# Down and output projections as seven products with tokens as the weights of TensorE

## The chip, the cores and the metric

The kernel runs on one core of one Trainium2 chip. The metric is device time in microseconds (us) of one execution. Engines are named as in the profile: PE is TensorE (PEld its weight loads), DVE is VectorE, ACT is ScalarE, POOL is GpSimd, SP the engine that issues the DMAs. A "product" below is one matmul instruction of PE: it multiplies a *stationary* block (128x128, loaded as weights) by a *moving* block of 128 rows and up to 512 columns and adds the result to a bank of PSUM.

## The reference

One transformer block on 2048 tokens of width 640, attention and a gated MLP side by side on the same normalised input:

```python
xn = layernorm(x)
q, k, v = split(xn @ wqkv)                 # 32 heads of 20
p = softmax(mask(q k^T / sqrt(20)))        # causal, window of 256 keys
o = p v                                    # heads joined: 640 columns
h = gelu(xn @ w_gate) * (xn @ w_up)        # 1728 columns
out = x + o @ wo + h @ w_down
```

All is float32. The kernel keeps float32 accuracy on PE by splitting each operand into a high part (rounded to the type fp32r) and a low part (the rest), and adding three products: high by high, high by low, low by high. One "term" below is such a set of three.

## The kernel before, in words

The work has three stages, one after the other in time, with PE busy through all of them.

- **Stage 1 (to about 658 us)**: layer norm, q, k and v, attention, and the first gate and up tiles as filler. Each unit of attention leaves its unnormalised output in DRAM (`od[c]`, 640 rows by 512 tokens, `av_unit`, L492) and the softmax sums in `sd[c]` (32 heads by 512 tokens). There are four chunks `c` of 512 tokens.
- **Stage 2 (658 to 843 us)**: the other gate and up tiles, `gate_up_pair` (L846), which already forms its products from sums of blocks (seven products in place of eight). Its list `extra` takes small jobs that are hung in between its product groups (`more(i)`, L852). Results go to DRAM as `hd[f]`: tile f (128 hidden features) by 512 tokens. During this stage the softmax sums are inverted and split into three bfloat16 parts (`norm_items`, L997), which are kept in SBUF as `rp`.
- **Stage 3 (843 us to the end)**: down and output projection. The loop of L1092 goes over 4 chunks of 512 tokens and, within a chunk, over 14 tiles of `hd` and 5 tiles of `od`, 19 steps in all. The *weights are stationary*: for each of the five blocks of 128 output columns, `terms` (L940) multiplies 128x128 blocks of `wd` or `wo` (high and low) by 512 moving token columns and adds into one of five PSUM banks (`ps_w`). The output is thus transposed (columns by tokens), and the host turns it back.

What sets the order in stage 3: SP issues the DMAs in the program's order (`MANUAL_OUT`, L41); the other engines are scheduled. A step n is loaded three steps ahead (`load_step`, L906, tile `hr`) and split two steps ahead (`split_step`, L920): ACT makes the high part of 128x512 (L932), POOL the low part (L934). For an attention step PE first spreads the inverted sums over the rows by a product with 0/1 weights `sel` (L925, `ps_b`), DVE multiplies (L927), ACT takes the high part (L928), DVE the low part (L929). The weights of the 19 tiles are loaded one a step during the first chunk and split once, ACT high (L76) and DVE low (L77); they then stay in SBUF. At the end of a chunk DVE adds the input `xt` and SP stores (L961, L962).

The last two weight tiles' preparation in stage 2 (`down`, L1018) and the splits of steps 0 and 1 are hung into the last gate and up tile (f = 12) by `second` (L1072 to L1074).

Of the kernel before, what the change touches and what calls it, by code (L numbers as in the profile page):

```python
# [9 lines left out]
F32 = mybir.dt.float32  # L10
# [9 lines left out]
C = 512  # L20
# [4 lines left out]
NF = 14  # L25
# [9 lines left out]
NDA = 2  # L35
# [8 lines left out]

@with_exitstack
def block_kernel(ctx, tc, x, xt, wqk, wv, wo, wgu, wd, wdl, out):
# [16 lines left out]
    xh = xp.tile([128, KT, S], F32R, name="xh")  # L63
    xl = xp.tile([128, KT, S], F32R, name="xl")
# [5 lines left out]
    td = [{i: dram.tile([128, 2, C], F32, name=f"td{p}{i}") for i in (1, 2, 3, 4)} for p in range(NC // 2)]  # L70
    hd = [dram.tile([NC, 128 if f < NF - 1 else 64, C], F32, name=f"hd{f}") for f in range(NF)]
# [21 lines left out]
    wrp = ctx.enter_context(tc.tile_pool(name="wrp", bufs=2))  # L93
    wp = ctx.enter_context(tc.tile_pool(name="wp", bufs=2))
    hp = ctx.enter_context(tc.tile_pool(name="fb", bufs=1, reuse_waits="tile"))
# [394 lines left out]
    def av_unit(u):  # L490
# [12 lines left out]
        for j in range(4):  # L503
            r0 = 80 * g + DH * j
            nc.sync.dma_start(od[c][r0:r0 + DH, :], ob[32 * j:32 * j + DH, :])
# [228 lines left out]
    cp = p2.enter_context(tc.tile_pool(name="cp", bufs=1, reuse_waits="tile"))  # L734
# [6 lines left out]
    wds, wos = {}, {}  # L741

    def load_w(src):
        raw = wrp.tile([128, KT, 128], F32, name="wr", tag="wr").rearrange("p k m -> p (k m)")
        nc.sync.dma_start(raw, src)
        return raw

    def load_d(f):
        return load_w(wd[f * 128:(f + 1) * 128, :] if f < NF - 1 else wdl)

    def norm_load(c):
        rc = cp.tile([128, 128], F32, name="rc", tag="rc", bufs=2)
        nc.sync.dma_start(rc, sd[c].rearrange("h (a t) -> (h a) t", a=4))
        return rc

    def norm(rc):
        rb = cp.tile([128, 3, 128], BF, name="rb", tag="rb", bufs=2)
        nc.vector.reciprocal(rc, rc)
        for i in range(3):
            nc.vector.tensor_copy(rb[:, i, :], rc)  # L760
            if i < 2:
                nc.vector.tensor_tensor(out=rc, in0=rc, in1=rb[:, i, :], op=OP.subtract)
        return rb

    def norm_store(c, rb):
        rp = cp.tile([96, C], BF, name=f"rp{c}")
        for i in range(3):
            nc.sync.dma_start(rp[32 * i:32 * i + 32, :], rb[:, i, :])
        rps.append(rp)

    rps = []
    sel = cp.tile([96, 768], BF, name="sel")[:, 0:D]
    nc.gpsimd.memset(sel[0:32], 1.0)
    nc.gpsimd.affine_select(out=sel[0:32], in_=sel[0:32], pattern=[[1, D]], compare_op=OP.is_ge,
                            fill=0.0, base=0, channel_multiplier=-DH)
    nc.gpsimd.affine_select(out=sel[0:32], in_=sel[0:32], pattern=[[-1, D]], compare_op=OP.is_ge,
                            fill=0.0, base=DH - 1, channel_multiplier=DH)
# [20 lines left out]
    def load_xs(p, i):  # L798
        t = cp.tile([128, 2, C], F32, name="ht", tag="ht", bufs=3)
        nc.sync.dma_start(t, td[p][i])  # L800
        return t
# [100 lines left out]
    raws, rts = {}, {}  # L902
    steps = [(c, n) for c in range(NC) for n in [("d", f) for f in range(NF)] + [("o", k) for k in range(KT)]]
    steps = [(c, kind, i) for c, (kind, i) in steps]

    def load_step(n):  # L906
        c, kind, i = steps[n]
        if kind == "o":
            raw = rp3.tile([128, C], F32, name="o", tag="o", bufs=3)
            nc.sync.dma_start(raw, od[c][i * 128:(i + 1) * 128, :])  # L910
        else:
            raw = cp.tile([128, C], F32, name="hr", tag="hr", bufs=4)
            if i < NF - 1:
                nc.sync.dma_start(raw, hd[i][c])
            else:
                for p in (0, 64):
                    nc.sync.dma_start(raw[p:p + 64], hd[i][c])
        raws[n] = raw

    def split_step(n):  # L920
        c, kind, i = steps[n]
        raw = raws.pop(n)
        if kind == "o":
            ps = psb.tile([128, C], F32, name="ps_b", tag="b")
            nc.tensor.matmul(ps, sel[:, i * 128:(i + 1) * 128], rps[c], start=True, stop=True)  # L925
            t = rp3.tile([128, 2, C], F32R, name="ot", tag="ot", bufs=4)
            nc.vector.tensor_tensor(out=raw, in0=ps, in1=raw, op=OP.mult)  # L927
            nc.scalar.activation(t[:, 0, :], raw, AF.Copy)  # L928
            nc.vector.tensor_tensor(out=t[:, 1, :], in0=raw, in1=t[:, 0, :].bitcast(F32), op=OP.subtract)  # L929
        else:  # L930
            t = cp.tile([128, 2, C], F32R, name="ht", tag="ht", bufs=3)
            nc.scalar.activation(t[:, 0, :], raw, AF.Copy)  # L932
            if i < NF - 1:
                nc.gpsimd.tensor_tensor(out=t[:, 1, :], in0=raw, in1=t[:, 0, :].bitcast(F32), op=OP.subtract)  # L934
            else:
                nc.vector.tensor_tensor(out=t[64:128, 0, :], in0=raw[64:128], in1=t[64:128, 0, :].bitcast(F32),  # L936
                                        op=OP.subtract)
        rts[n] = t

    def terms(ns, pss):  # L940
        work = []
        for n in ns:
            c, kind, i = steps[n]
            t = rts.pop(n)
            wh, wl = (wds if kind == "d" else wos)[i]
            work += [(wh, t[:, 0, :]), (wl, t[:, 0, :])]
            if (kind, i) != ("d", NF - 1):
                work.append((wh, t[:, 1, :]))
        c, kind, i = steps[ns[0]]
        first = (kind, i) == ("d", 0)  # L950
        last = steps[ns[-1]][1:] == ("o", KT - 1)
        for m in range(KT):
            ms = slice(m * 128, (m + 1) * 128)
            for j, (w, r) in enumerate(work):
                nc.tensor.matmul(pss[m], w[:, ms], r, start=first and j == 0, stop=last and j == len(work) - 1)  # L955
            if last:
                final = (c, m) == (NC - 1, KT - 1)
                ot = rp3.tile([128, C], F32, name="out", tag="out", bufs=KT)
                for p in ((0, 256), (256, 512)) if final else ((0, C),):
                    p = slice(*p)  # L960
                    nc.vector.tensor_tensor(out=ot[:, p], in0=pss[m][:, p], in1=xts[c, m][:, p], op=OP.add)  # L961
                    nc.sync.dma_start(out[ms, c * C + p.start:c * C + p.stop], ot[:, p])  # L962

    def get_xt(c, m):
        a = xts[c, m] = rp3.tile([128, C], F32, name="xts", tag="xts", bufs=KT)
        nc.sync.dma_start(a, xt[m * 128:(m + 1) * 128, c * C:(c + 1) * C])
# [30 lines left out]
    def norm_items(c):  # L997
        st = {}

        def n1():  # L1000
            st["rc"] = rc = norm_load(c)

        def n2():
            rc = st["rc"]
            st["rb"] = cp.tile([128, 3, 128], BF, name="rb", tag="rb", bufs=2)
            nc.vector.reciprocal(rc, rc)
            nc.vector.tensor_copy(st["rb"][:, 0, :], rc)

        def n3():
            rc, rb = st["rc"], st["rb"]  # L1010
            for i in (1, 2):
                nc.vector.tensor_tensor(out=rc, in0=rc, in1=rb[:, i - 1, :], op=OP.subtract)
                nc.vector.tensor_copy(rb[:, i, :], rc)
            norm_store(c, rb)

        return n1, n2, n3

    def down(j):  # L1018
        def fn():
            wds[j] = split(cp, dw.pop(j), [128, D], f"wd{j}", nc.gpsimd)  # L1020
        return fn

    dw, norms, carry = {}, {}, []
# [11 lines left out]
    for j, f in enumerate(range(NFA, NF - 1)):  # L1035
# [13 lines left out]
        if j == 1:  # L1049
            first[3].append(lambda: [nc.vector.tensor_copy(sel[i:i + 32], sel[0:32]) for i in (32, 64)])  # L1050
        if end:
            for i in range(NDA):
                dw[i] = load_d(i)
                first[1 + 2 * i].append(down(i))
        else:
# [96 lines left out]
```

## Time and profile before

| what | value |
|---|---|
| time, median of 3 runs | 1110.18 us (1110.1 to 1110.83) |
| time of the profiled execution | 1110.84 us |
| its span, first to last instruction | 1109.1 us |
| granted TensorE clock | 0.999 |
| PE busy | 1092.0 us (98%) |
| DVE, ACT, POOL busy | 600.4, 468.8, 410.5 us |
| stage 3: first product of `ps_w` starts, last one ends | 843.46, 1105.39 us |
| DVE busy from 900 to 1090 us | 33.4 of 190 us |
| moved by DMA | 133.09 MB, 120 GB/s on average |

The profile is of the one execution in the third line and all times within it count from the span's start. A row of groups reads: line, engine, operation, output from inputs, shape, count, then busy us and mean ns of one, then the engine's idle time just before them with what ended it. A row of the timeline reads: start, length, engine, line, operation, names, shape, count, and in brackets the idle time before it. Rows with the count x3 are three instructions run together, from the first's start to the last's end. An instruction's length on PE, DVE and ACT is from start to the end of its result; the next can start a little before that, so the distance of two starts (the pace) is shorter than the length.

### The profile page before, as it was taken

The numbers are of one execution on the slowest core, as the hardware profiler recorded it, in microseconds if no ns is written. First come the engines' busy times: TensorE is split into PE (matmuls) and PEld (weight loads), VectorE is DVE, ScalarE is ACT, GpSimd is POOL, SyncE is SP. The second block draws the span as 40 slices with busy tenths as digits, with TensorE's granted clock in tenths as the row PEclk, the third lists the DMA queues.
The fourth block names the chain that finished last, engine by engine and source line by source line (L and its number), as shares of the span: only waits on it lengthen the run. The fifth ranks groups of instructions, "written<-read, shape, count | busy, mean of one in ns | idle before, by whom it ended". The sixth has DMA issues, their size and how long they took to land.

```text
span 1109.1 us, 19240 instructions
## 1 busy us (share of the span) xinstructions
PE 1092.0 (98%) x6778; PEld 830.3 (75%) x6778; DVE 600.4 (54%) x1646; ACT 468.8 (42%) x952; POOL 410.5 (37%) x570
## 2 busy tenths in 40 slices
PE   8999999999999999999999999999999999999998
PEld 7877666666688767666666768888888778788886
DVE  7766667565665666666666636666554250311203
ACT  4434655556554556555554554232233322211111
POOL 5045624557635535653534341111113313221230
PEclk9999999999999999999999999999999999999999
DMA  5643343546433233443323125222125745152421
GB/s 202 192 135 92 101 147 93 145 116 195 139 98 96 75 119 105 151 128 120 113 91 108 61 93 167 70 93 84 66 74 194 219 132 167 48 180 72 157 95 66
DMA packets 76144, 133.09 MB, mean 120 GB/s; under 512 B 12800, under 2 KB 33664, under 8 KB 76048
## 3 DMA queue, kind: packets, MB, share of 16 engines
q1 hardware_dynamic: 76048, 131.87, 38.0%
q8 instruction: 53, 0.87, 0.3%
q14 instruction: 43, 0.35, 0.1%
HBM read 86.31 MB, written 44.83 MB: 118 GB/s over the span
## 4 chain that ended last, share of the span: by engine, by line
PE 85%; DVE 5%; issue 3%; DMA 2%; ACT 2%; POOL 1%; SPq 1%; DVEq 0%; POOLq 0%; ACTq 0%
PE ps_d L84 23%; PE ps_w L955 19%; PE ps_g L864 14%; PE ps_o L498 7%; PE ps_e L476 7%; PE ps_m L424 7%; PE ps_v L84 5%; DVE junk L426 2%; PE ps_g L84 1%; POOL ht L934 1%; ACT P L478 1%; DVE xi L142 1%; PE ps_t L159 1%; DMA hr<-hd 1%; DVE r L219 0%
## 5 line engine op out<-in xcount | busy, mean ns | idle before, releaser
L426 DVE CUSTOM_DVE_ANT_0 junk<-ps_m,mask 128x384 bf16<-128x384 f32 (+2 forms) x512 | 271.6, 530 | 177.2 <-PE ps_m L424 135.9
L478 ACT ACTIVATE P<-ps_e 128x512 f32<-128x512 f32 (+2 forms) x384 | 197.6, 568 | 63.7 <-PE ps_e L476 57.5
L484 POOL TENSOR_SCALAR_AFFINE_SELECT P<-P 128x512 f32<-128x512 f32 x128 | 84.0, 656 | 176.3 <-ACT P L478 169.3
L934 POOL TENSOR_TENSOR ht<-hr,ht 128x512 fp32r<-128x512 f32 x52 | 69.9, 1351 | 173.6 <-ACT ht L932 173.6
L84 PE MATMUL ps_d<-xh,wql 128*128 128x512 f32 x430 | 129.2, 410 | 0.0
L84 PE MATMUL ps_d<-xl,wqh 128*128 128x512 f32 x430 | 128.6, 408 | 0.0
L84 PE MATMUL ps_d<-xh,wqh 128*128 128x512 f32 x430 | 128.5, 409 | 0.0
L424 PE MATMUL ps_m<-ks,qs 120*128 120x128 bf16 (+1 forms) x704 | 121.1, 275 | 3.8 <-DVE mx L426 1.8
L476 PE MATMUL ps_e<-qs,ks 122*128 122x128 bf16 (+2 forms) x704 | 113.1, 277 | 1.5 <-ACT P L478 0.8
L476 PEld LDWEIGHTS <-ks 122*128 122x128 bf16 x704 | 50.2, 98 | 55.1 <-issue 44.5
L84 PEld LDWEIGHTS ps_d<-xh,wql 128*128 128x128 f32 x430 | 77.9, 189 | 15.7 <-issue 2.3
L84 PEld LDWEIGHTS ps_d<-xl,wqh 128*128 128x128 f32 x430 | 78.2, 188 | 14.9 <-issue 0.6
L932 ACT ACTIVATE ht<-hr 128x512 fp32r<-128x512 f32 x56 | 35.0, 628 | 126.1 <-PE ps_w L955 80.7
L84 PEld LDWEIGHTS ps_d<-xh,wqh 128*128 128x128 f32 x430 | 77.7, 189 | 14.1 <-ACT xh L167 0.3
L424 PEld LDWEIGHTS <-qs 120*128 120x128 bf16 x704 | 62.1, 98 | 33.1 <-issue 14.4
L487 POOL TENSOR_SCALAR_AFFINE_SELECT P<-P 128x512 f32<-128x512 f32 x112 | 72.5, 659 | 37.4 <-ACT P L478 37.4
L498 PE MATMUL ps_o<-P,v 128*32 128x384 f32 (+2 forms) x1408 | 84.3, 386 | 0.0
L207 POOL TENSOR_TENSOR pt<-r,pt 128x512 bf16<-128x512 f32 x40 | 46.8, 1171 | 79.1 <-ACT pt L206 64.8
L498 PEld LDWEIGHTS ps_o<-P,v 128*32 128x32 f32 x1408 | 40.1, 110 | 39.5 <-issue 29.2
L936 DVE TENSOR_TENSOR ht<-hr,ht 64x512 fp32r<-64x512 f32 x4 | 2.8, 690 | 112.3 <-ACT ht L932 112.3
L502 ACT ACTIVATE ob<-ps_o 128x512 f32<-128x512 f32 x32 | 19.1, 597 | 103.9 <-PE ps_o L498 50.7
L77 POOL TENSOR_TENSOR wql<-wr,wqh 128x640 fp32r<-128x640 f32 x9 | 14.5, 1615 | 129.5 <-PE ps_g L864 106.1
(273 smaller groups left out, 2036.3 us busy)
## 6 DMA issues: line engine op xcount, KB each, us to landing
hd<-he SPq DMA_DIRECT2D x52, 256.0 KB
hr<-hd SPq DMA_DIRECT2D x52, 256.0 KB
wr<-wgu SPq DMA_DIRECT2D x27, 320.0 KB
qs<-qd SPq DMA_DIRECT2D x32, 240.0 KB
ks<-kd SPq DMA_DIRECT2D x32, 240.0 KB
xi<-x SPq DMA_DIRECT2D x16, 320.0 KB
qs<-qd SPq DMA_DIRECT2D x32, 160.0 KB
ks<-kd SPq DMA_DIRECT2D x32, 160.0 KB
```

What stands on the lines that cost most here:

```text
L84: nc.tensor.matmul(ps, a(k), b(k), start=n == 0, stop=n == 3 * nk - 1)
L207: nc.gpsimd.tensor_tensor(out=pt[:, l, :], in0=r, in1=pt[:, 1, :], op=OP.subtract)
L424: nc.tensor.matmul(ps[:, lo:hi], lh, rhs, start=True, stop=True)
L426: nc.vector.tensor_tensor_reduce(out=junk[:, 0:n], in0=ps[:, 0:n], in1=mask[:, 384 - n:384], scale=1.0, scalar=NEG, op0=OP.add, op1=OP.max ...
L476: nc.tensor.matmul(ps[:, col:col + n], k[0:QROWS, j, kc:kc + 128], q[0:QROWS, j, q0:q0 + n], start=True, stop=True)
L478: nc.scalar.activation(pt[:, j, lo:hi], ps[:, lo:hi], AF.Exp, scale=SCALE)
L484: nc.gpsimd.affine_select(out=a, in_=a, pattern=[[0, 4], [1, 128]], compare_op=OP.is_ge, fill=0.0, base=0, channel_multiplier=-1)
L487: nc.gpsimd.affine_select(out=a, in_=a, pattern=[[0, 4], [-1, 128]], compare_op=OP.is_ge, fill=0.0, base=-1, channel_multiplier=1)
L498: nc.tensor.matmul(o[32 * j:32 * j + 32, q0:q0 + n], v[:, w0_:w0_ + 32], pt[:, j, col:col + n], start=i == 0, stop=i == len(todo) - 1, ski ...
L864: nc.tensor.matmul(ps, i, j, start=first and n == 0, stop=n == len(work) - 1, skip_group_check=True)
L934: nc.gpsimd.tensor_tensor(out=t[:, 1, :], in0=raw, in1=t[:, 0, :].bitcast(F32), op=OP.subtract)
L955: nc.tensor.matmul(pss[m], w[:, ms], r, start=first and j == 0, stop=last and j == len(work) - 1)
```

## The change

Stage 3 is rewritten; stages 1 and 2 issue the same work up to the last gate and up tile, but for what is named here.

**Products.** Now the *tokens* are stationary and the weights move, 320 columns at a time, so the output comes out as tokens by columns and needs no turning. A step is a pair of token blocks (2 x 128 tokens, 8 pairs `p`) and a "quad" `k`: two of the 18 feature tiles (13 of `wd` and 5 of `wo`, arranged as 9 quads) by two halves of 320 output columns. A quad is a 2x2 by 2x2 block product. In pair 0 it is done plainly, with 8 block products (24 PE instructions); in pairs 1 to 7 by seven block products (21 PE instructions) on sums and differences of the blocks. Tile 13 (64 rows) is the extra step "e", 8 instructions. Seven PSUM banks hold the products until the pair's end, when `drain` combines them.

**Weights.** Each quad is kept in SBUF as blocks ("b", high and low, 128x1280 each) and as sums ("t", high and low). `b0` to `b3` are made while the last gate and up tile runs and just after it, the other blocks and all sums during pair 0 (`prepare`). Raw quads pass through three staging buffers (`stg`); a raw quad is overwritten by its sums. The quads 0 to 3 are loaded a second time for their sums.

**Tokens.** For each step of pairs 1 to 7 DVE forms four sums of 128x128, ACT two high parts, DVE two low parts. POOL does no splitting there, and multiplies the attention rows by the inverted sums instead.

**Softmax sums.** In stage 2 only the reciprocal is taken and written to DRAM (`rd`); stage 3 reads it back four times over 128 partitions (`load_rb`). For this, heads and dimensions change places in the rows of `od` and `wo`. The products with `sel` are gone.

**Order.** In stage 3 all engines keep the program's order (ACT, DVE, PE, POOL and SP).

```diff
+    borrow = {7: 0, 3: 4}
+    def fetch(q, pool, tag, bufs):
...
+            t = pool.tile([128, 4, HD], F32, name="stg", tag=tag, bufs=bufs)
+            nc.sync.dma_start(t, wdo[q].rearrange("p k (h n) -> p (k h) n", h=2))
...
+    def sums_quad(q):
+        t, = staged[q]
+        sub(t[:, 0], t[:, 1], t[:, 0])
+        sub(t[:, 1], t[:, 3], t[:, 1])
+        sub(t[:, 3], t[:, 3], t[:, 0])
+        sub(t[:, 2], t[:, 2], t[:, 3])
...
     def split_step(n):
...
+        for i in range(2):
+            if 2 * k + i >= NF - 1:
+                a = raw[:, 2 * i:2 * i + 2].rearrange("p a t -> p (a t)")
+                nc.gpsimd.tensor_tensor(out=a, in0=a, in1=rbs[c][:, t0:t0 + 256], op=OP.mult)
+        if p == 0:
+            nc.scalar.activation(hi[:, 0:4], raw, AF.Copy)
+            sub(lo[:, 0:4], raw, hi[:, 0:4].bitcast(F32))
+            return
+        s = rp3.tile([128, 4, 128], F32, name="ss", tag="ss", bufs=2)
+        nc.scalar.activation(hi[:, 0:3], raw[:, 1:4], AF.Copy)
+        sub(s[:, 0], raw[:, 0], raw[:, 2], OP.add)
+        sub(s[:, 1], s[:, 0], raw[:, 1])
+        sub(s[:, 2], raw[:, 1], raw[:, 0])
+        sub(s[:, 3], raw[:, 3], s[:, 1])
+        nc.scalar.activation(hi[:, 3:7], s, AF.Copy)
+        sub(lo[:, 0:3], raw[:, 1:4], hi[:, 0:3].bitcast(F32))
+        sub(lo[:, 3:7], s, hi[:, 3:7].bitcast(F32))
...
     def terms(n, ps, begin, end):
...
+        if p == 0:
+            for bank, a, b in ((2, (1, 3), 0), (3, (1, 3), 1), (4, (0, 2), 0), (8, (0, 2), 1)):
+                mul(bank, three(a[0], wb, b) + three(a[1], wb, b + 2))
+            return
+        for bank, a, w, b in ((1, 0, wb, 0), (2, 2, wb, 2), (4, 1, None, 2), (5, 3, None, 0), (6, 4, None, 3),
+                              (7, 5, None, 1), (3, 6, wb, 3)):
+            mul(bank, three(a, w, b))
...
+    def drain(p, ps, xt):
...
+        nc.scalar.activation(a, b[1], AF.Copy)
+        add(1, 1, b[2])
+        add(1, 1, a, nc.gpsimd)
+        store(1, 1)
+        add(2, 1, b[4])
+        add(1, 2, b[5])
+        add(2, 2, b[5])
+        sub(a, b[6], a, OP.add)
+        add(1, 2, a)
+        sub(a, b[7], a, OP.add)
+        add(1, 2, b[3])
+        store(1, 2)
+        add(2, 1, a)
+        store(2, 1)
+        add(2, 2, a)
+        store(2, 2)
...
+            fetch(0, cp, "stg", 1)
+            fetch(1, None, "", 0)
+            second[0].append(lambda: quad(0, nc.vector))
+            second[1].append(lambda: [split_step(0), quad(1, nc.gpsimd), fetch(2, cp, "stg", 1), load_step(2)])
+            second[2].append(lambda: [split_step(1), quad(2, nc.vector), fetch(3, None, "", 0)])
...
+    def prepare(n):
+        if n == 0:
+            high_quad("b", 3)
+            low_quad("b", 3, nc.vector)
+            load_rb(0)
+            nc.scalar.activation(w13[:, 0], raw13, AF.Copy)
+            sub(w13[:, 1], raw13, w13[:, 0].bitcast(F32))
+        if 1 <= n <= 5:
+            high_both(n + 3)
+            high_quad("t", n + 3)
+            low_quad("t", n + 3, nc.gpsimd)
+        if 6 <= n <= 9:
+            q = n - 6
+            sums_quad(q)
+            high_quad("t", q)
+            low_quad("t", q, nc.gpsimd)
+        if n in follow:
+            stage(follow[n], n == 3 or n == 5)
+    follow = {1: 7, 3: 8, 2: 0, 4: 1, 5: 2, 6: 3}
...
+    for n, (p, k) in enumerate(steps):
...
+        if n + 4 < len(steps):
+            load_step(n + 4)
         if n + 2 < len(steps):
             split_step(n + 2)
+        prepare(n)
+        terms(n, ps, i == 0, i == NQD)
...
+        if i == NQD:
+            drain(p, ps, xr)
```

The lists `second` are hung into the last gate and up tile (f = 12, chunks 2 and 3). `high_both` makes a quad's b high (ACT), b low (DVE) and sums (DVE). `borrow` puts `t7` and `t3` into the block that pairs 1 to 7 don't use in four b quads each. `low_quad` is one subtraction of 128x1280 (four of 128x320 for `t7` and `t3`), `high_quad` one copy of the same size. The split tiles of the tokens (`at`) have three buffers, so step n + 2 is split once step n - 1 has been multiplied.

More of the change, by code (lines that the diff above doesn't have):

```diff
@@ L70, in block_kernel @@
     td = [{i: dram.tile([128, 2, C], F32, name=f"td{p}{i}") for i in (1, 2, 3, 4)} for p in range(NC // 2)]
+    rd = [dram.tile([H, C], F32, name=f"rd{c}") for c in range(NC)]
     hd = [dram.tile([NC, 128 if f < NF - 1 else 64, C], F32, name=f"hd{f}") for f in range(NF)]
@@ L740, in block_kernel, with norm_items, n1, n2 @@
     psg = pg.enter_context(tc.tile_pool(name="psg", bufs=2, space=PSUM, reuse_waits="tile"))
[L741 to L777, printed above, removed]
+    def norm_items(c):
+        st = {}
+        def n1():
+            st["rc"] = c2.tile([128, 128], F32, name="rc", tag="rc", bufs=2)
+            nc.sync.dma_start(st["rc"], sd[c].rearrange("h (a t) -> (h a) t", a=4))
+        def n2():
+            nc.vector.reciprocal(st["rc"], st["rc"])
+        def n3():
+            nc.sync.dma_start(rd[c].rearrange("h (a t) -> (h a) t", a=4), st["rc"])
+        return n1, n2, n3
     def gate_up(ws, c, tag):
@@ L900, in gate_up_pair @@
         nc.sync.dma_start(hd[f][2 * p], h1)
-    raws, rts = {}, {}
-    steps = [(c, n) for c in range(NC) for n in [("d", f) for f in range(NF)] + [("o", k) for k in range(KT)]]
-    steps = [(c, kind, i) for c, (kind, i) in steps]
-    def load_step(n):
[L907 to L918, printed above, removed]
+    quads, staged, raws, ats = {}, {}, {}, {}
@@ new lines, in block_kernel, with new_quad, slots @@
+    place = {("b", 0): "xh1", ("b", 1): "xl1", ("b", 2): "xh0", ("b", 3): "xl0",
+             ("t", 0): "xh2", ("t", 1): "xl2", ("t", 2): "xh3", ("t", 8): "xl3"}
+    borrow = {7: 0, 3: 4}
+    def new_quad(kind, q):
+        tag = place.get((kind, q))
+        quads[kind, q] = (xp if tag else rp3).tile([128, 2, 4, HD], F32R, name=f"w{kind}{q}", tag=tag or f"w{kind}{q}")
+    def slots(kind, q):
+        if kind == "t" and q in borrow:
+            return [(quads["b", borrow[q] + i], slice(1, 2), slice(i, i + 1)) for i in range(4)]
+        if (kind, q) not in quads:
+            new_quad(kind, q)
+        return [(quads[kind, q], slice(0, 4), slice(0, 4))]
@@ new lines, in sub, with t_slot @@
+    def sub(o, i, j, op=OP.subtract):
+        nc.vector.tensor_tensor(out=o, in0=i, in1=j, op=op)
+    def sums_quad(q):
[4 more added lines that the diff above has]
+        sub(t[:, 2], t[:, 2], t[:, 3])
+    def t_slot(q, i):
+        if q in borrow:
+            return quads["b", borrow[q] + i], 1
+        return quads["t", q], i
+    NP = S // 256
+    steps = []
+    for p in range(NP):
+        ks_ = list(range(NQD))
+        if p % 2:
+            ks_ = ks_[4:] + ks_[:4]
+        steps += [(p, k) for k in ks_[:4] + ["e"] + ks_[4:]]
@@ L920, in split_step, with load_rb @@
+    def load_rb(c):
+        rbs[c] = cp.tile([128, C], F32, name="rb", tag="rb")
+        for i in range(4):
+            nc.sync.dma_start(rbs[c][32 * i:32 * i + 32], rd[c])
     def split_step(n):
-        c, kind, i = steps[n]
+        p, k = steps[n]
         raw = raws.pop(n)
[L923 to L962, printed above, removed]
@@ L995, in split_later_xs @@
         return fn
[L997 to L1023, printed above, removed]
+    norms, carry = {}, []
     def start_norm(c):
@@ L1048, in block_kernel @@
             second[0].append(split_later_xs(4))
[L1049 to L1055, printed above, removed]
+        if not end:
             nxt_w, sums = [], {}
@@ L1089, in block_kernel @@
-    psb = p3.enter_context(tc.tile_pool(name="psb", bufs=2, space=PSUM, reuse_waits="tile"))
-    late = [(wds, f, f"wd{f}") for f in range(NDA, NF)] + [(wos, k, f"wo{k}") for k in range(KT)]
-    held = []
-    for n, (c, kind, i) in enumerate(steps):
-        if (kind, i) == ("d", 0):
-            pss = [psn.tile([128, C], F32, name="ps_w", tag="w") for _ in range(KT)]
-        if late:
-            for d, j, name in (late.pop(0),):
-                raw = load_d(j) if d is wds else load_w(wo[j * 128:(j + 1) * 128, :])
-                d[j] = split(rp3, raw, [128, D], name, nc.vector)
-        if n + 3 < len(steps):
-            load_step(n + 3)
-        if kind == "d" and 3 <= i < 3 + KT:
-            get_xt(c, i - 3)
+    rp3 = p3.enter_context(tc.tile_pool(name="rp3", bufs=1, reuse_waits="tile"))
@@ new lines, in block_kernel @@
+    follow = {1: 7, 3: 8, 2: 0, 4: 1, 5: 2, 6: 3}
+    raw13 = rp3.tile([128, D], F32, name="xr", tag="xr")
+    nc.sync.dma_start(raw13, wdl)
+    for n in (4, 5, 6):
+        stage(n, n == 6)
+    load_step(3)
+    for n, (p, k) in enumerate(steps):
+        i = n % (NQD + 1)
+        if i == 0:
+            ps = {b: psn.tile([128, C], F32, name=f"ps_{b}", tag=f"b{b}") for b in (1, 2, 5, 3, 6, 4, 7, 8)}
+        if i == 3:
+            xr = get_x(p)
+        if i == 8 and p % 2 and p + 1 < NP:
+            load_rb(p // 2 + 1)
+        if n + 4 < len(steps):
+            load_step(n + 4)
```

157 lines of the change are left out of this document (126 added, 31 removed).

## The prediction, on record before the run

> **What bounds the kernel now.** I read the page's chain first, then that chain in order of time. PE carries 85% of it, and in stage 3 it never waits: 225 products in 51.02 us are one every 0.227 us.
>
> ```profile
> PE 85%; DVE 5%; issue 3%; DMA 2%; ACT 2%; POOL 1%; SPq 1%; DVEq 0%; POOLq 0%; ACTq 0%
> ```
> ```profile
> 900.50 0.23 PE ps_b L925
> 900.74 51.02 PE ps_w L955 x225
> 951.76 0.23 PE ps_b L925
> ```
>
> The other engines have room there (DVE is busy 33.4 of 190 us), so fewer or shorter products pay at once, as long as nobody makes PE wait. The new product has 320 columns and its own weight load. The kernel has this form already, in v's projection; the timeline shows runs of five and of three (start, length), the second view a single one (least/median/greatest ns):
>
> ```profile
> 70.43 0.90 PE L84 MATMUL ps_v<-wvh,xl 128*128 128x320 f32 x5
> 366.11 0.60 PE L84 MATMUL ps_v<-wvh,xl 128*128 128x320 f32 x3
> ```
> ```profile
> L84 PE MATMUL ps_v<-wvh,xl x160: 302/309/449, 21.7 to 367.5; 128*128 128x320 f32 x160
> ```
>
> (0.90 - 0.31)/4 and (0.60 - 0.31)/2 give a pace of 0.147 us. Then I read how DVE and POOL get along, in the timeline around the last gate and up tile:
>
> ```profile
> 831.45 1.57 POOL L77 TENSOR_TENSOR wd1l<-wr,wd1h 128x640 fp32r<-128x640 f32 x1 [4.06 <-ACT wd1h L76]
> 832.03 1.53 DVE L897 TENSOR_TENSOR he<-qp,hr 128x512 f32<-128x512 f32 x1
> 833.48 0.68 DVE L899 TENSOR_TENSOR he<-u,hr 128x512 f32<-128x512 f32 x1
> ...
> 838.26 1.30 POOL L934 TENSOR_TENSOR ht<-hr,ht 128x512 fp32r<-128x512 f32 x1 [5.25 <-ACT ht L932]
> 838.29 0.69 DVE L867 TENSOR_TENSOR qp<-ps_g,q 128x512 f32<-128x512 f32 x1 [2.72 <-PE ps_g L864]
> ```
>
> L897 reads two operands from SBUF. It starts while POOL works and takes 1.53 us, ending 0.54 after POOL (833.02); L899, the same work alone, takes 0.68. L867, with one operand in PSUM, is not held up by POOL (0.69). So a DVE instruction on two SBUF operands and a POOL instruction exclude each other. Last, the durations, from the groups kept apart by shape (count, busy us, mean ns):
>
> ```profile
> L796 DVE TENSOR_TENSOR xl<-ht,xh 128x1024 fp32r<-128x1024 f32 x8 | 9.8, 1221 | 3.0 <-ACT xh L795 2.9
> L795 ACT ACTIVATE xh<-ht 128x1024 fp32r<-128x1024 f32 x8 | 8.4, 1052 | 0.4 <-DMA ht<-td 0.4
> L529 POOL TENSOR_TENSOR wql<-wr,wqh 128x128 fp32r<-128x128 f32 x95 | 40.9, 466 | 27.0 <-ACT wqh L524 20.6 <-DMA od<-ob 6.2
> L77 POOL TENSOR_TENSOR wd0l<-wr,wd0h 128x640 fp32r<-128x640 f32 x1 | 1.6, 1569 | 15.8 <-ACT wd0h L76 15.8
> ```
>
> Straight lines through these and the 128x512 rows (DVE 0.68, ACT 0.63) give my estimates. DVE: 0.28 (128 columns), 0.49 (320), 0.55 (384), 1.49 (1280); in a row without dependence each starts 0.08 before the last ends (833.48 against 833.56), so the paces are 0.20, 0.41, 0.47, 0.60 (512), 1.41. ACT: 1.27 (1280). POOL: 0.73 (256), 2.9 (1280). A load is readable 3.0 us after its issue (834.57 to 837.55, half a MB queued), and the fullest two microseconds moved 380 GB/s:
>
> ```profile
> 852.00:854.00 2.00, 2.00 (x11) 1.65 (x10) 0.46 (x1) 1.23 (x2) 0.00 (x0) 1.00 1.03 380
> ```
>
> **The sum, part by part.** All times below count from 843.46, where stage 3 starts now. It ends on PE at 1105.39, so lasts 261.9 us.
>
> *Products.* Pair 0: 9 x 24 + 8 = 224; pairs 1 to 7: 9 x 21 + 8 = 197 each. 224 x 0.147 = 32.9 us, 7 x 197 x 0.147 = 202.7 us, together 235.6. **Gain 26.3 us**, if PE never waits.
>
> Here a rule of the Trainium skill speaks against the change. "TensorE: Matmul & The Clock Gate", section "The mechanism", says that a weight load runs beside running products only if it is for other rows of the array, and section "LDWEIGHTS (loading the stationary operand)" prices a load of 128 columns at 107 ns; by the two, an estimate, the 1603 products would take 171 us more. The trace does not agree: whole blocks with a load each run at 0.147.
>
> *Entry.* The raw quad 0 is issued after two stores (833.59, 834.19) and four h loads, at 836.1, behind 0.5 MB, and lands about 840.1 (-3.3). In the changed queue order ACT has b0's high part before `q`, and DVE b0's low part before the addition that PE's third group waits for; both were free before. PE waits there and reaches stage 3 at about +7. Further, `gelu` of g2 now stands on ACT behind b3's high part, whose raw data needs the buffer that POOL's b1 low frees: the last stores of `hd` leave at +10 instead of +2.5. Behind them SP issues wdl, three quads and step 3's tile: 2.55 MB, 6.5 us at 390 GB/s, 2 us of latency, 0.8 of issue. Step 3 is split at 20.6, PE is through steps 0 to 2 at 17.7 and starts step 3 at 20.6. **+7 and +3.**
>
> *Pair 0.* PE needs 3.5 us a step, the preparation far more. For quads 4 to 8 the orders are: ACT b high, t high, next tile's high part; DVE b low, sums, next tile's low part; POOL t low. From the end of one quad's sums: t high 1.3, POOL 2.9, in which DVE's low part of the next tile must stand still, then that low part 0.6, b low 1.4, four sums 1.7 (with a hand-off): **8.0 us a quad**. In "e" DVE waits the same way. For the last two steps POOL's two multiplications of the attention rows (1.4) stand behind its t low, and ACT's high part (0.6) behind them: 8.6 us. Step by step, PE can start: e 28.8; step 5 36.7; 6 44.6; 7 53.6 (t7 in four pieces, one multiplication); 8 64.2; 9 72.9; end 76.5. That is 36.5 us of waiting, the 3 of step 3 among them. As a check without any order: between +20 and +73, DVE's two-operand work (five b low 7, six quads' sums 10, six low parts 4) and POOL's (six t low 18, five multiplications 4) are 43 us that exclude each other. SP's queue has the reloads of `stg` before later tiles, but they come while these waits last.
>
> *Pair 1.* Its first step is split at 79.3, but banks 2, 3, 4 and 8 come free only when `drain` of pair 0 has run, and DVE has the sums of quads 2 and 3 and step 11's split before it: 90.1. Step 10 ends at 92.0, eight steps and e take 25.9, step 12 waits 2.1 more (POOL's t3 and multiplications): 120.0, so **+14.5**.
>
> *Pairs 2 to 7.* DVE a pair: 9 x (4 x 0.20 + 0.47 + 0.60) + e 0.35 + 11 x 0.41 = 21.7, some 2 for hand-offs, and POOL's 4.5 (five multiplications, one addition): 28.2 of PE's 28.96. The bounds are 28.96, and 31.9 with lengths instead of paces (27.4) plus POOL; I take 29.2, near the paces, since PSUM reads don't exclude POOL. The new waits on banks fit: DVE reads bank 2 two microseconds before the pair's last product ends. 6 x 29.2 = 175.2, **+1.5**, PE ends at 295.2.
>
> *Tail.* After the last product DVE has five more instructions, 2.3 us instead of 0.79, then one store more in the queue, 0.4: **+1.9**.
>
> *At nothing:* fewer normalisation jobs on DVE in stage 2, the changed row order in `od` (same row sizes), `sel` and its 20 products (within the 26.3). Their cover is PE's unbroken work.
>
> Sum: -26.3 + 7 + 36.5 + 14.5 + 1.5 + 1.9 = +35.1. The profiled execution took 1110.84, within the runs shown (median 1110.18): **1146 us**.
>
> **Rivals.**
> - *POOL and DVE don't exclude each other at these shapes.* Then the quad's cycle is t high 1.3, ACT 0.6, low part 0.6, b low 1.4, sums 1.7 = 5.6, saving 2.4 on some five cycles and about 2 at pair 1: 1132. Against it: the row above.
> - *DVE bounds the pairs.* At 31.9 a pair, 6 x 2.7 = 16 more: 1162. It decides once DVE's waits for ACT and POOL exceed 0.8 us a pair beyond those counted. For it: small slack.
> - *Faster: preparation stays hidden in pair 0.* If one quad's work fits into a step of 3.5 us, only the entry and the tail remain: 1110.84 - 26.3 + 10 + 1.9 = 1096. It turns when PE's waits stay under 24.4 us in all (I count 59.5). For it: three quads are ready at the start, and POOL's t is needed only in pair 1. Against: DVE's b low and sums alone are 3.1 us a quad, ACT's two copies 2.5, in a chain.
> - *Weight loads show.* The load's row is 0.188 us; uncovered, 1603 of them cost 301 us, under which the other waits vanish: about 1390. The Trainium skill's rule above is this rival; v's rows leave it 1%.
>
> **How the numbers follow.** Forecast 0.68, no exclusion 0.13, DVE bound 0.12, hidden 0.05, loads 0.01, no change 0.01. Time 1146. The range goes below the first rival by some loads landing earlier, and above the second by some landing later: 1126 to 1166. A measurement here tells about 0.2% (2.2 us) from no change. Faster 0.05, same 0.01, slower 0.94.
>
> **What would show it.** PE's rows of 320 columns at 0.147; PE idle about 36 us between 850 and 920, ended by DVE's low parts `at`, eight microseconds apart; POOL's t low at 2.9 with a DVE row of 3 us beside it; bank waits at the first boundary; later pairs 29 to 30 us apart. Wrong if pair 0 ends before 900, or if later pairs take over 31.

## The result, and the profile after

The changed kernel takes 1149.24 us (median of four runs, 1147.74 to 1152.38) against 1110.51 in the same runs for the kernel before: 1.0349 times as long, with a 95% interval of 1.0325 to 1.0374. The profiled execution took 1152.38 us (span 1150.7), 41.5 more than the one of before. It is the slowest of the four. 1.3 of the 41.5 lie ahead of PE's first new wait: in the traces the last product of stage 2 before that wait starts at 840.49, its counterpart in the kernel before at 839.16. The four runs below that leave everything up to there as it is have it between 839.23 and 841.12, so 1.3 is no more than executions differ by.

The page's chain still names PE first, but DVE, issue and DMA have grown:

```profile
PE 82%; DVE 7%; issue 4%; DMA 3%; ACT 2%; POOL 1%; SPq 1%; DVEq 0%; POOLq 0%; ACTq 0%
```

The timeline on PE shows what became of the products. These are the two closing products of step "e", once in each pair, so their distance is the length of a pair (they go to an eighth PSUM bank, beside the seven of the block products):

```profile
1013.68 0.46 PE L1030 MATMUL ps<-w,he 128*128 128x320 f32 x2
...
1042.62 0.46 PE L1030 MATMUL ps<-w,he 128*128 128x320 f32 x2
...
1071.58 0.46 PE L1030 MATMUL ps<-w,he 128*128 128x320 f32 x2
...
1100.51 0.46 PE L1030 MATMUL ps<-w,he 128*128 128x320 f32 x2
```

28.95 us for 197 products is 0.147 each, the pace that v's projection had, weight load included. So pairs 2 to 7 run at PE's limit and **the gain of the products is there**. The windows (length, then busy us and count of PE, PEld, DVE, ACT and POOL, the granted clock, the DMA share and GB/s) show where it was given back: PE is busy all of the later stretch, and 45.8 of 75 us in pair 0.

```profile
855.00:930.00 75.00, 45.84 (x219) 41.86 (x217) 40.11 (x51) 20.74 (x25) 24.72 (x15) 0.75 0.42 140
...
1000.00:1100.00 100.00, 100.00 (x683) 99.82 (x682) 85.45 (x232) 36.56 (x69) 15.21 (x19) 1.00 0.48 145
```

The waits of PE from 835 to 1000 us (total, times, longest), 45 us in all:

```profile
PE ps L1023 <- ACT at L1003: 19.2, 5, 4.8
PE ps L1023 <- DVE xr L1053: 10.2, 1, 10.2
PE ps L1023 <- DVE at L944: 6.6, 4, 2.6
PE ps_g L858 <- DVE qp L861: 6.0, 1, 6.0
PE ps L1023 <- DVE he L944: 3.2, 1, 3.2
```

And this is one cycle of pair 0 in the timeline of all engines. L941 on POOL is t low, L944 the low part of the tokens (`at`) and the sums (`stg`), L941 on DVE b low, L931 on ACT the high parts of a quad:

```profile
882.92 2.89 POOL L941 TENSOR_TENSOR wt<-stg,wt 128x1280 fp32r<-128x1280 f32 x1 [5.29 <-ACT wt L931]
...
883.39 2.97 DVE L944 TENSOR_TENSOR at<-hr,at 128x512 fp32r<-128x512 f32 x1 [1.85 <-ACT at L1003]
...
886.28 1.48 DVE L941 TENSOR_TENSOR wb<-stg,wb 128x1280 fp32r<-128x1280 f32 x1
...
886.41 5.75 PE L1023 MATMUL ps<-wb,at 128*128 128x320 f32 x24 [2.37 <-DVE at L944]
...
887.80 2.07 DVE L944 TENSOR_TENSOR stg<-stg 128x320 f32<-128x320 f32 x4
889.90 1.27 ACT L931 ACTIVATE wt<-stg 128x1280 fp32r<-128x1280 f32 x1 [5.38 <-DVE stg L944]
891.08 0.61 ACT L1003 ACTIVATE at<-hr 128x512 fp32r<-128x512 f32 x1
891.25 2.90 POOL L941 TENSOR_TENSOR wt<-stg,wt 128x1280 fp32r<-128x1280 f32 x1 [5.44 <-ACT wt L931]
...
891.73 2.97 DVE L944 TENSOR_TENSOR at<-hr,at 128x512 fp32r<-128x512 f32 x1 [1.86 <-ACT at L1003]
```

DVE's low part of the tokens takes 2.97 us where it takes 0.69 elsewhere (at 913.64, for one). It starts 0.47 after POOL's instruction and ends 0.55 after it. PE's 24 products wait for its end. Then b low, the sums, ACT's copies, and the next pair of POOL and DVE: 8.34 us from one `at` to the next, of which PE works 3.5 (5.75 here, at a lower clock).

This is the cycle of quads 5 and 6. DVE is held up in this way five times (rows of 2.9 to 3.0 us from 875.00 to 934.39). In the steps with attention rows it isn't: there POOL's multiplications (L1001) stand behind its t low, ACT's high part waits for them (11.0 us in three waits), and PE for ACT:

```profile
908.71 2.88 POOL L941 TENSOR_TENSOR wt<-stg,wt 128x1280 fp32r<-128x1280 f32 x1 [6.84 <-ACT wt L931]
911.54 1.41 POOL L1001 TENSOR_TENSOR hr<-hr,rb 128x256 f32<-128x256 f32 x2
...
912.98 0.63 ACT L1003 ACTIVATE at<-hr 128x512 fp32r<-128x512 f32 x1 [4.35 <-POOL hr L1001]
...
913.66 5.87 PE L1023 MATMUL ps<-wb,at 128*128 128x320 f32 x24 [4.84 <-ACT at L1003]
```

The stage in the terms of the prediction, from the starts and ends of PE's rows (the length of the stretch less its products at 0.147):

| stretch | predicted | measured |
|---|---|---|
| 26.3 us less of products | -26.3 | -26.3 |
| ahead of PE's first new wait | 0 | +1.3 |
| entry: from the last product before the wait to stage 3 | +7 | 13.4 - 4.3 = +9.1 |
| pair 0, with step 3's wait (4.2) | +36.5 | +41.6 |
| pair 1 | +14.5 | +13.9 |
| pairs 2 to 7 | +1.5 | 0 |
| tail | +1.9 | +1.6 |
| sum | +35.1 | +41.2 (execution: +41.5; the rest is rounding) |

### The profile page after: what moved, and what is told of

It reads as the page before. It is cut to its first block, busy times and chain, and to the rows that moved or that the text cites. A ratio compares the mean times of both kernels' runs of the same rounds, so it can differ in the third digit from the quotient of the medians.

```text
span 1150.7 us, 20894 instructions
## 1 busy us (share of the span) xinstructions
PE 1088.6 (95%) x7241; PEld 871.0 (76%) x7241; DVE 757.4 (66%) x2064; ACT 512.4 (45%) x1034; POOL 403.7 (35%) x577
## 4 chain that ended last, share of the span: by engine, by line
PE 82%; DVE 7%; issue 4%; DMA 3%; ACT 2%; POOL 1%; SPq 1%; DVEq 0%; POOLq 0%; ACTq 0%
PE ps_d L99 22%; PE ps L1023 18%; PE ps_g L858 14%; PE ps_o L514 7%; PE ps_e L492 7%; PE ps_m L440 6%; PE ps_v L99 5%; DVE junk L442 1%; PE ps_g L99 1%; DVE at L944 1%; DMA stg<-wdo 1%; DVE stg L944 1%; ACT P L494 1%; DMA xi<-x 1%; DVE xi L158 1%
## 5 line engine op out<-in xcount | busy, mean ns | idle before, releaser
L1023 PE MATMUL ps<-wb,at 128*128 128x320 f32 x951 | 162.2, 324 | 36.3 <-ACT at L1003 19.2
L1023 PEld LDWEIGHTS ps<-wb,at 128*128 128x128 f32 x951 | 151.5, 199 | 40.4 <-ACT at L1003 20.8
L1023 PE MATMUL ps<-wt,at 128*128 128x320 f32 x588 | 96.1, 313 | 0.0
L1023 PEld LDWEIGHTS ps<-wt,at 128*128 128x128 f32 x588 | 89.6, 191 | 0.5 <-DVE m L944 0.2
L944 DVE TENSOR_TENSOR at<-hr,at 128x384 fp32r<-128x384 f32 (+1 forms) x72 | 51.0, 708 | 34.6 <-ACT at L1003 26.0
L1012 ACT ACTIVATE at<-ss 128x512 fp32r<-128x512 f32 x63 | 39.7, 630 | 72.3 <-DVE ss L944 72.1
```

Source lines behind the costliest of these rows:

```text
L944: nc.vector.tensor_tensor(out=o, in0=i, in1=j, op=op)
L1023: nc.tensor.matmul(ps[bank][:, 0:HD], a, b, start=begin and j == 0 and (k != "e"), stop=end and j == last, skip_group_check=True)
```

## The experiments

The theory: pair 0 is set by a serial chain of preparation (sums, t high, t low, low part of the tokens, b low), longer by the time in which POOL's t low keeps DVE out. Its rivals: the loads set it; POOL's work is free; PE's low clock lengthens the chain; the new form has costs of its own in every pair.

**t low from POOL to DVE.**

```diff
-            low_quad("t", n + 3, nc.gpsimd)
+            low_quad("t", n + 3, nc.vector)
...
-            low_quad("t", q, nc.gpsimd)
+            low_quad("t", q, nc.vector)
```

> The low parts of the nine sums (t low) go from POOL to DVE, 1.41 us each where POOL took 2.9; nothing else changes. If the chain of preparation with DVE and POOL excluding each other sets pair 0: the cycle from sums to sums becomes t high 1.3, t low 1.4, low part of the tokens 0.6, b low 1.4, sums 2.1 = 6.9 instead of 8.3; the attention steps lose POOL's t low in front of their multiplications as well (11.1 and 9.0 become 7 to 8); some 18 us in all, about 1132, and no DVE row of 2.9 is left. If loads set it: within 2 us of 1149, with PE's waits ended by loads.

Measured: 1139.44, ratio 1.0256 [1.0221, 1.0291]. DVE's timeline there, one cycle from sums to sums:

```profile
876.75 2.07 DVE L944 TENSOR_TENSOR stg<-stg 128x320 f32<-128x320 f32 x4
880.16 1.49 DVE L941 TENSOR_TENSOR wt<-stg,wt 128x1280 fp32r<-128x1280 f32 x1 [1.33 <-ACT wt L931]
881.57 0.68 DVE L944 TENSOR_TENSOR at<-hr,at 128x512 fp32r<-128x512 f32 x1
882.17 1.49 DVE L941 TENSOR_TENSOR wb<-stg,wb 128x1280 fp32r<-128x1280 f32 x1
883.69 2.07 DVE L944 TENSOR_TENSOR stg<-stg 128x320 f32<-128x320 f32 x4
```

The 2.97 is gone, and the cycle is 6.94 as expected. The whole gain is 10 us and not 18, since I counted the later cycles at 9 to 11 us (PE's step distances); from sums to sums they were 7.3 to 9.0 in the changed kernel, and fell to 5.4 to 8.4. The loads are not what set the pace: taking POOL off the chain moved it. DVE waits 1.3 us for ACT's t high in each cycle of this form, so what sets the pace is the order of the chain's own steps.

**No low parts of the sums at all.** The line is left out instead of moved, to price POOL's part alone.

```diff
+            low = wb[:, 1, b]
...
-            return [(t[:, 0, a], w[:, 0, b]), (t[:, 1, a], w[:, 0, b]), (t[:, 0, a], w[:, 1, b])]
+            return [(t[:, 0, a], w[:, 0, b]), (t[:, 1, a], w[:, 0, b]), (t[:, 0, a], low)]
...
-            low_quad("t", n + 3, nc.gpsimd)
...
-            low_quad("t", q, nc.gpsimd)
```

> The changed kernel with the low parts of the sums left out (the products read the low parts of the b blocks in their place), all else as it is. POOL has only its multiplications left in pair 0. If POOL's low parts cost their time through excluding DVE, the cycle from sums to sums falls to t high 1.3, high and low part of the tokens 1.1, b low 1.4 and sums 2.1 = 5.9, under that of the run with the low parts on DVE (6.9): nine cycles, about 1129. If POOL's low parts ran beside DVE's work for nothing: no change, 1149.

Measured: 1130.0, ratio 1.0182 [1.016, 1.0205]. DVE's sums there:

```profile
868.12 2.07 DVE L944 TENSOR_TENSOR stg<-stg 128x320 f32<-128x320 f32 x4
...
874.52 2.07 DVE L944 TENSOR_TENSOR stg<-stg 128x320 f32<-128x320 f32 x4
...
881.13 2.07 DVE L944 TENSOR_TENSOR stg<-stg 128x320 f32<-128x320 f32 x4
```

The cycle is 6.4 to 6.6 us where it was 8.3 (5.9 was expected), and the boundary of the pairs comes sooner as well. **POOL's low parts cost 19 us in all (1149.2 - 1130.0)**, so they were not free. Both of their effects are gone from pair 0: `at` takes 0.69 us in every step, and ACT's high part no longer waits for POOL. How the 19 us divide between the two isn't shown. (The staging buffers also come free sooner here; but from 868.7 to 945 us of the changed kernel no wait of PE, ACT, DVE or POOL was ended by a load.)

**No preparation of the sums at all.**

```diff
         low_quad("b", q, nc.vector)
-        sums_quad(q)
...
-            high_quad("t", n + 3)
-            low_quad("t", n + 3, nc.gpsimd)
-        if 6 <= n <= 9:
-            q = n - 6
-            sums_quad(q)
-            high_quad("t", q)
-            low_quad("t", q, nc.gpsimd)
...
-        if q in borrow:
-            return quads["b", borrow[q] + i], 1
-        return quads["t", q], i
+        return quads["b", q], i
```

> Left out: the sums of the weights, their high and low parts (the products of pairs 1 to 7 read the b blocks in their place); all loads stay, the repeated ones of quads 0 to 3 too. If the preparation of the sums sets pair 0: DVE has 1.4 + 0.6 us a step left, PE's 3.5 covers it, and pairs 0 and 1 run at PE's pace; entry 10.4, step 3's wait 4 with some 2.5 of low clock behind it, and the tail 1.7 remain: 1110.8 - 26.3 + 18.6 = 1103, give or take 4. If loads set it, most of the wait stays: over 1125.

Measured: 1107.66, ratio 0.9978 [0.9961, 0.9994], 41.6 us under the changed kernel and 0.7 above the range that I expected, all loads kept. Only three waits of PE are left from 830 to 1000 us:

```profile
PE ps_g L858 <- DVE qp L861: 5.1, 1, 5.1
PE ps L1021 <- ACT at L1001: 5.0, 1, 5.0
PE ps L1021 <- DVE xr L1051: 3.1, 1, 3.1
```

By the starts of PE's rows, 14 us are left of the 55.5 that pairs 0 and 1 cost in the table: 8.3 up to step "e" (step 3's wait and the lower clock behind it), the rest around the boundary of the pairs. So the sums' preparation explains the other 41 us. Loads at this pace are no limit: from 870 to 880 us they moved 332 GB/s with PE busy throughout.

**Quad 0 asked for sooner; then step 3's tokens first too.** The first is `fetch(0, cp, "stg", 1)` moved ahead of the first pair of gate and up groups. The second adds:

```diff
-            second[2].append(lambda: [split_step(1), quad(2, nc.vector), fetch(3, None, "", 0)])
+            second[2].append(lambda: [split_step(1), load_step(3), quad(2, nc.vector), fetch(3, None, "", 0)])
...
-    load_step(3)
...
-            load_rb(0)
...
+        if n == 2:
+            load_rb(0)
```

> Raw quad 0 is asked for one pair of gate and up groups sooner, so that it has landed when ACT comes to it. The 6 us of PE's wait in the last gate and up tile and the low clock behind it (4 us) go. If what follows is set by the last stores of hd and the loads behind them, step 3's wait grows in return: those stores move by 4 us only, since ACT's gelu still stands behind the high part of b3; about 1145. If the entry adds in full: 1139.

> The changed kernel with the edits of the loads alone (raw quad 0 sooner, step 3's tokens ahead of the weights, the inverted sums' load two steps later). The entry's wait goes, and the chain of preparation starts when quad 4 lands instead of behind step 3's tokens: some 10 us sooner, 1139; pair 0's cycles of 8 us stay as they are. If the entry were the main cost, PE's waits in pair 0 would shrink as well: under 1125.

Measured: 1145.87, ratio 1.0325 [1.0295, 1.0356], and 1139.47, 1.0269 [1.0249, 1.0289]. With the first edit PE's wait in the last gate and up tile is gone and stage 3 starts at 843.37, but step 3 waits 6.28 instead of 4.02 for its tokens, which stand in SP's queue behind the late stores of `hd`:

```profile
860.37 6.54 PE L1023 MATMUL ps<-wb,at 128*128 128x320 f32 x24 [6.28 <-ACT at L1003]
```

With both edits the first sums start at 857.25 instead of 871.29, 14 us sooner (2 of which lie ahead of the entry), and pair 0's cycles stay as they are (8.35 from 872.37 to 880.72 on PE). Both times are as expected. By the medians the first edit gives 3.4 us and the two together 9.8, so most of the entry's price comes back only once the load behind it is moved as well.

**Filler products in PE's waits.**

```diff
+    def fill(n, t, wb, ps):
+        m = {2: 24, 3: 24, 4: 36, 5: 24, 6: 24, 7: 42, 8: 36, 9: 12, 10: 60}.get(n, 0)
+        for j in range(m):
+            nc.tensor.matmul(ps[1][:, 0:HD], t, wb, start=j == 0, stop=j == m - 1,
+                             skip_group_check=True)
```

> Filler products of 320 columns (into a bank that pair 0 doesn't use) run on PE where it waits in pair 0 and at the first boundary: 282 more products, so that the granted clock stays up. If the preparation sets the pace, the clock of PE is worth only what stands behind the last wait (steps 9 and 10): 1 to 3 us faster, about 1147. If the low clock itself lengthens pair 0, through the three buffers of the split tokens: 8 us faster or more, about 1140. If the filler gets in the way: slower.

Measured: 1149.49, ratio 1.0344 [1.032, 1.0369], the same as the changed kernel. The clock stayed at full speed:

```profile
855.00:930.00 75.00, 67.52 (x442) 64.76 (x441) 40.32 (x50) 20.77 (x25) 25.16 (x15) 1.00 0.42 140
```

67.5 us of busy PE and a clock of 1.00 where the changed kernel had 45.8 and 0.75, with no gain that the runs can tell. The rival's 8 us are out, so the low clock in pair 0 is a result of the waits and not their cause. The 1 to 3 us that I expected are neither shown nor out: the interval is 2.7 us to either side.

**Plain products in all pairs** (`p < 9` for each `p == 0`, no sums; both edits of the loads).

> All eight pairs take plain products, with no sums at all, and the two edits of the loads. If the gain of the later pairs comes from seven products in place of eight: 8 x 224 products of 0.147 are 263.4 us where the kernel before has 261.9, with 1.3 of entry, 1.7 of tail and 4 to 6 of waits in pair 0: 1110.8 + 1.5 + 1.3 + 1.7 + 5 = 1120, each pair 32.9. If a part of the gain lies in the tokens being stationary: under 1112.

Measured: 1118.51, ratio 1.0066 [1.005, 1.0081]. Its pairs on PE:

```profile
897.45 1.34 PE L1024 MATMUL ps<-w,he 128*128 128x320 f32 x8
...
930.31 1.33 PE L1024 MATMUL ps<-w,he 128*128 128x320 f32 x8
...
963.16 1.33 PE L1024 MATMUL ps<-w,he 128*128 128x320 f32 x8
```

32.86 a pair, eight of them 262.9, where the kernel before takes 261.9. So stationary tokens with 320 columns give and cost next to nothing in products, and 3.9 us a pair come from the seven products.

**Two plain pairs, with and without the edits of the loads.** The sums are taken out of `high_both`, and spread:

```diff
-        if p == 0:
+        if p < 2:
...
+        if n in late:
+            high_quad("t", late[n])
+            low_quad("t", late[n], nc.vector)
...
-    follow = {1: 7, 3: 8, 2: 0, 4: 1, 5: 2, 6: 3}
+    late = {6: 0, 8: 1, 10: 2, 11: 4, 13: 5, 14: 6, 16: 8, 17: 7, 19: 3}
+    follow = {1: 7, 2: 8, 3: 0, 4: 1, 5: 2, 6: 4, 8: 5, 10: 6, 11: 8, 13: 7, 14: 3}
...
+        if n in late:
+            sums_quad(late[n])
```

> Pairs 0 and 1 both take plain products (27 products more: 4.0 us), and the sums with their high and low parts are spread over steps 6 to 19, their low parts on DVE; the raw quads are loaded a second time for it. Raw quad 0 is asked for one pair of gate and up groups sooner, and step 3's tokens ahead of the weights that follow. If preparation that doesn't fit beside one pair is the cause: DVE's work for it, 5 b low, 9 sums, 9 t low and 20 token splits, is 7 + 19 + 13 + 13 = 52 us of the 66 that two plain pairs take, so that little waits: 1110.8 - 26.3 + 4.0 + 1.7 + 0 to 6 = 1090 to 1096, faster than before. If the new form has waits of its own at its pairs or loads: over 1105.

> The same without the two edits of the loads: the entry (10.4) and step 3's wait (4, with some 2.5 of low clock behind it) stay: about 1093 + 16 = 1109, give or take 4. If the entry is hidden under what follows, nearer to 1095.

Measured: with the edits 1110.44, ratio 1.0005 [0.9995, 1.0016]; without 1117.3, 1.0069 [1.0049, 1.0089]. The first is 39 us under the changed kernel, 6.9 of them by the edits of the loads (9.8 in the changed kernel), but it missed my range by 14 us and the second by 4. PE still waits 13.6 us in the first, in nine waits of up to 2.3 us and a longer one at the end of pair 1 (with 2.74 us for nine products behind it, at a lower clock):

```profile
923.07 0.60 PE L1024 MATMUL ps<-wt,at 128*128 128x320 f32 x3
929.05 2.74 PE L1024 MATMUL ps<-wt,at 128*128 128x320 f32 x9 [5.38 <-DVE xr L1058]
```

```profile
922.51 2.07 DVE L945 TENSOR_TENSOR stg<-stg 128x320 f32<-128x320 f32 x4
...
926.82 1.69 DVE L942 TENSOR_TENSOR wb<-stg,wb 128x320 fp32r<-128x320 f32 x4
928.42 1.68 DVE L1058 TENSOR_TENSOR xr<-ps,xr 128x320 f32<-128x320 f32 x4
```

The drain (L1058) frees the bank, and DVE has the sums of quad 3 and their low parts ahead of it. A sum of DVE's busy time (52 of 66 us) was no measure: it has an order, and the drain was last in it.

**The same, tuned.** Quads 3 and 7 stay plain in pair 2 as well, their sums move behind the drain, the others a step earlier, and each quad's reload behind the next tokens' load.

```diff
+    def plain(p, k):
+        return p < 2 or p == 2 and k in (3, 7)
...
+        if p == 2:
+            ks_ = [0, 1, 3, 7, 2, 4, 5, 6, 8]
...
+    late = {5: 0, 7: 1, 9: 2, 10: 4, 12: 5, 13: 6, 15: 8, 25: 7, 30: 3}
+    follow = {1: (7,), 2: (8,), 3: (0,), 4: (1,), 5: (2, 4), 7: (5,), 9: (6,), 10: (8,), 12: (7,), 13: (3,)}
...
+        for q in follow.get(n - 1, ()):
+            stage(q, (n, q) in ((4, 0), (6, 4), (11, 8)))
```

> As the one with two plain pairs and the two edits of the loads, with three more: quads 3 and 7 stay plain in pair 2 too (6 products more, 0.9 us), so that their sums move past the drain of pair 1 into pairs 2 and 3, where DVE is busy 85%; the sums of the others start one step sooner; each repeated load of a quad is issued behind the next step's tokens. If the 5.4 us in which PE waits for the drain behind the sums, and the loads of attention tokens behind those of the quads, are what was missing there: 1110.4 - 5.4 - 2 (low clock behind it) - 3 + 0.9 = 1101. If DVE's work is too much for two pairs in any order, the waits come back in pairs 1 to 3: 1108 or more.

Measured: 1107.52, ratio 0.9971 [0.9961, 0.9982], **0.3% under the kernel before**: a small gain, but the interval leaves out 1. Expected was 1101, and 1108 or more if DVE's work is too much in any order; with 9.5 us of waits left the run lies near the second. The wait for the drain is gone from PE's waits of 830 to 1110 us, but one of 4.5 is new, where quad 0's sums stand on DVE ahead of a token split, while the quad is still loading:

```profile
PE ps L1030 <- DVE at L949: 7.8, 5, 4.5
PE ps L1030 <- DVE he L949: 0.7, 1, 0.7
PE ps L1030 <- ACT m L1085: 0.6, 1, 0.6
PE ps L1030 <- DVE m L949: 0.4, 1, 0.4
```

> As the tuned one, but the sums of quad 0 stand one step later on DVE, behind the token split that they held up while their reloaded quad was still on its way (PE waited 4.45 us there, DVE 3.9 for the DMA). If that wait was only a matter of order: 1107.5 - 3 to 4 = 1104. If the loads of that stretch (0.9 of the DMA's time) hold PE there anyway: 1106 to 1108.

With quad 0's sums one step later (`6: 0` in `late`, quad 4's reload with it) that wait is gone, others came in its place (6.6 us in seven pieces for `at`, the longest 1.7), and the time is 1108.21, ratio 0.9975 [0.9966, 0.9985]: no difference from the run above. So the wait was not only a matter of order; what holds PE there instead isn't shown.

## Why the prediction was right, point by point

- *Products, -26.3.* Right: 28.95 us a pair, and the plain pairs' 32.86, are 0.147 a product with a load each. The row of v's projection held for this form, and not the Trainium skill's rule on weight loads that I had weighed against it. (The section with that rule also names loads into a background weight buffer as running beside products, which I had left out.)
- *Entry, +7.* Mechanism right: PE waits 5.98 us for DVE's `qp`, behind ACT's high part of quad 0, which waits for its load; the wait is gone in the run that asks for quad 0 sooner.

```profile
842.68 1.27 ACT L931 ACTIVATE wb<-stg 128x1280 fp32r<-128x1280 f32 x1 [7.91 <-DMA stg<-wdo]
...
843.99 1.49 DVE L941 TENSOR_TENSOR wb<-stg,wb 128x1280 fp32r<-128x1280 f32 x1 [7.08 <-ACT wb L931]
...
846.12 0.68 DVE L861 TENSOR_TENSOR qp<-ps_g,q 128x512 f32<-128x512 f32 x1
```

  It cost +9.1 in the profiled execution, but +6.8 to +7.4 in the four runs with the same entry (t low on DVE, no t low, no sums, filler), so +7 was the right size. That is luck in part: the step "PE waits there and reaches stage 3 at about +7" has all of it as waiting and leaves out what the wait does to the clock. In those four runs some 5 us are waiting and 1.6 to 2.3 the lower clock behind it. In the profiled execution PE stood for 6.1 us, and the 15 products of 512 columns behind it took 6.3 us (0.43 each at first) instead of 3.4, 2.9 us more:

```profile
840.26 0.61 PE L858 MATMUL ps_g<-xl,s3h 128*128 128x512 f32 x2
846.86 1.22 PE L858 MATMUL ps_g<-xh,s4h 128*128 128x512 f32 x2 [5.98 <-DVE qp L861]
847.88 1.06 PE L858 MATMUL ps_g<-xh,s4l 128*128 128x512 f32 x2
...
852.57 0.77 PE L858 MATMUL ps_g<-xl,wqh 128*128 128x512 f32 x2
853.18 0.40 PE L858 MATMUL ps_g<-xh,wqh 128*128 128x512 f32 x1
...
853.88 10.72 PE L1023 MATMUL ps<-wb,at 128*128 128x320 f32 x72
```

- The Trainium skill has a rule for this that the prediction didn't use ("TensorE: Matmul & The Clock Gate", section "What's actually happening"): after about 3.4 us without work PE's clock is halved, and it comes back after as long of steady work. The trace agrees in kind (0.43 against 0.227 after a wait of 5.98); the slow stretch here was about 6 us, and 3.1 in the run with t low on DVE.
- *Step 3, +3, and pair 0, +36.5 with it.* Mechanism right: the first cycles, from sums to sums, are 8.2 to 8.4 us where I had 8.0, and the later ones longer (9.0), as forecast. 41.6 us in the place of 36.5: step 3 waited 4.2 (4.02 in PE's list of waits, which counts from the end of the last product), and the last step's products took 5.0 us instead of 3.6, at a lower clock. The rest is in the cycles (the four sums 2.07 in the place of 1.7), though one step of PE came out shorter than forecast (7.8 for 9.0). That the sums' work is the cause was shown by leaving it out: some 41 of the 55.5 us of pairs 0 and 1 went. POOL's share of it is 19 us. One sign came out otherwise: "ended by DVE's low parts `at`" holds for 6.6 us of PE's waits, while 19.2 end with ACT's high part of the tokens.
- *The exclusion of DVE and POOL.* Right, and the rival without it (1132) is out: `at` 2.97 against 0.69. The Trainium skill states it as a lock ("SBUF — State Buffer", section "Who interferes with whom"): a DVE instruction with two SBUF inputs and a GpSimd instruction that reads SBUF don't run together, and the later one waits for the whole of the other. The trace agrees: the delayed row ends 0.55 us after POOL's.
- *Pair 1, +14.5.* Right: +13.9. The bank wait of 10.2 us is there (`xr` in PE's waits), behind the sums of quads 2 and 3.
- *Pairs 2 to 7, +1.5.* Too much: they cost nothing, since DVE is busy 85% there and PE never waits for it. The rival "DVE bounds the pairs" is out.
- *Hidden preparation (1096)* is out by the waits of 45 us, and *weight loads (1390)* by the pace.
- *Slips in the working.* DVE's 27.4 us a pair by lengths come to 27.0 from the lengths given, and the two microseconds of the kernel before that are shown as the fullest (380 GB/s) are not: 664 to 666 us moved 394, near the 390 that the sum uses. Neither changes the forecast.

The error of 3 us in the median (1146 against 1149.2) is a net one, and its smallness partly luck: by the table, step 3 and pair 0 cost 5.1 us more than forecast, pairs 1 to 7 and the tail 2.4 less, and the entry, by the other runs, about what was forecast.

## What to carry to other kernels

A saving on the bounding engine that needs preparation is paid in the stage that prepares, so cost that stage as a chain with an order, not as a sum of busy times: here seven pairs gained 3.9 us each, and the entry and the first two pairs lost 65. Work handed to an idle POOL isn't free if DVE reads two operands from SBUF at the time. And when a wait is removed, look at what stands behind it in the same queue: a part of the entry's wait moved to step 3's tokens, and that for quad 0's sums to other token splits, instead of going.

## What the runs showed of the hardware

- PE's granted clock fell to 0.50 from 880 to 890 us, where PE was busy 4.7 of 10 us, and rose to 0.98 in the next ten with 5.8. In pair 0 it cost less than the runs can tell (1149.49 us with the clock kept at 1.00, 1149.24 without), because the waits behind the slow products were longer; at the entry it cost 1.6 to 2.9 us in five executions, because PE itself was the limit there.
- A 128x320 product with its own weight load of 128 columns kept 0.147 us in every full pair, over 197 and 224 products in a row, while the loads' own rows show 0.188 us, more than the pace, so loads and products overlap. Whether any part of a load still shows isn't known: no run has the product without its load.
